# From block 13 on, score matmuls on 64x64 tiles that leave out the band's two empty quarters; an exp per key half; other due times

## The chip, the cores and the metric

The kernel runs on 1 core of one Trainium2 chip. The metric is device microseconds of that core for one execution. A core has TensorE (PE) for matmuls, VectorE (DVE), ScalarE (ACT), GpSimd (POOL) and SyncE (SP); POOL and SP issue the DMAs here. The profile names TensorE's weight loads apart, as PEld.

## The reference

Sliding-window attention with a linear distance bias, and a two-layer MLP with a squared ReLU on its result. B = 8, H = 8, S = 576, D = 64, window = 128; x is [4608, 512], the MLP is 512 -> 2048 -> 512.

```python
scores = scale * np.matmul(q, k.transpose(0, 1, 3, 2))
mask = (rel >= 0) & (rel < window)              # rel = query - key
scores = np.where(mask, scores - slope[h] * |rel|, -1e9)
attn = softmax(scores)
x = (attn @ v), heads side by side              # [4608, 512]
h = x @ w_in;  g = relu(h) ** 2;  out = g @ w_out
```

A block of 128 queries needs two blocks of keys: its own (keys not after the query) and the one before (keys less than 128 back). In the own block, keys 64..127 meet no query 0..63; in the block before, keys 0..63 meet no query 64..127. These are the band's two empty 64x64 quarters.

## The kernel before

**Blocks.** A batch has 576 tokens: four blocks of 128 and one of 64, 40 blocks in all, numbered m = 5 * b + kb. For each block, `load_block` (L338) loads k, q and v as bf16 with three POOL DMAs (L356) into the rings `kq` (8 buffers) and `vt` (8). `turn` (L388) transposes k and q into `kqT` (5 buffers): on TensorE for the blocks of `KQ_PE` (L425, with an evacuation by L373 on DVE or L375 on ACT), by a DMA transpose on SP's queue (L398) for the others.

**Scores.** `score` (L441) computes the scores transposed: keys on PSUM partitions, queries on columns. One head has contraction 64, so the two heads of a pair sit in the two row halves of the array. For each of the four pairs c, for each of the two key blocks, for each half, there is one 64-row matmul with 128 key columns as weights and 128 query columns as moving operand (L469): 16 matmuls a block. The 64-token last block of a batch is scored together with the first block of the next ("pair", 24 matmuls). The results go to four PSUM banks of pool A. A bank (`slot_s[i]`) takes two heads, and for each head 256 columns: key part 0 (block before), then part 1 (own). For each bank, ACT computes exp into a P buffer, 128 x 512 (L488), and DVE multiplies it with the mask exp(-slope * distance), zero outside the band (L496).

**Values.** `mix` (L500) multiplies P with v; a 65th column of ones gives the row sums (L516, 8 matmuls for each half of the heads, one bank each). DVE takes the reciprocal (L539) and normalizes into `x` (L544). x is transposed into `xT` on TensorE for the blocks of `X_PE` (L562), by a DMA transpose on SP (L554) for the others.

**MLP.** For each of nine groups g of 512 tokens, `fc_step` (L590) does 64 matmuls of 512 columns (L604) in steps of four, each step followed by ReLU on ACT (L613) and a square on DVE (L620); `t_part` (L655) does 64 matmuls with w_out (L665). A finished 128x512 tile is evacuated by ACT (L636) and stored by SP or POOL (L644). MLP matmuls use the four banks of pool B; scores, P times v and most transposes use the four banks of pool A.

**The order of work.** Every piece of work is a task with an engine, a planned cost, a key (due time), dependencies, and the slots that it takes and frees. `Plan.order` (L59) runs a list schedule over planned costs and fixes the order on each engine; the chip then runs each engine's list in order, waiting where data or a buffer is missing. A block's key is its place in the token stream less `AHEAD[m]` (L193, default `LEAD` or 0). `fill` (L712) puts matmuls on zeros (L705, L707) where the plan has TensorE idle in the first 26 us, `FILL` of the gap; `WARM` (L311) puts 24 ahead of all. `HOLD` and `OSB` (L202) say how long stores are held back and how many output buffers there are. Exp and mask take the key parts from the first one in use (`lo // 128`) to the last.

```python
at = 128 * i + 64 * part if pair and i == 0 else 128 * part          # L453
tm = plan.add({"PE": 220.0 + C * sum(max(w[2], 64) / 2.4 + 4 for w in work_of)}, due - 28, burst, ...)
te = plan.add({"ACT": act(cols)}, due - 28 + 3 * i, expo, [tm], [], [slot_s[i]])
```

Of the kernel before, what the change touches and what calls it, by code (L numbers as in the profile page):

```python
# [10 lines left out]
AF = mybir.ActivationFunctionType  # L11
ALU = mybir.AluOpType
# [158 lines left out]
def kernel(  # L171
    ctx: ExitStack, tc: tile.TileContext, q, k, v, moe_w_in, moe_w_out, out
):
    nc = tc.nc
# [5 lines left out]
    scale = 1.0 / (D ** 0.5)  # L180
# [4 lines left out]
    C = d_model // 128  # L185
# [4 lines left out]
    FIRST = "b0 b1 b2 i0 i1 i2 b3 i3 o0 b4 b5 o1 b6 b7 o2 o3 b8 b9"  # L190
    SPLIT = {0: [(0, 128), (128, 256), (256, 384), (384, 512)], 1: [(0, 192), (192, 512)]}
    EARLY = -80
    AHEAD = {10: -60, 1: 60, 4: 90, 9: -60, 5: -60, 0: -30, 12: 60, 11: 90, 2: 60, 8: 90, 7: 60, 6: 0, 3: -30, 24: 30, 14: 0, 18: 30, 25: 0, 23: 30, 16: -30, 13: 30, 21: 0, 19: -30}  # L193
    LEAD = 20

    KQ_PE = [0, 1, 2, 3, 4, 5, 6, 7, 8, 9]
    X_PE = [0, 1, 2, 3, 4, 5, 7, 8, 12, 17]
    WARM = 24
    FILL, UNTIL = 0.8, 26e3
    COLD = 0  # L200
    BANKS = {"A": 4, "B": 4}
    HOLD, OSB = 12, 14  # L202

    const = ctx.enter_context(tc.tile_pool(name="const", bufs=1))
    psum = ctx.enter_context(tc.tile_pool(name="psum", bufs=2, space=bass.MemoryType.PSUM))
# [3 lines left out]
    ident32 = const.tile([128, 128], FP32)  # L209
    kq32 = const.tile([128, 2, d_model], FP32)  # L210
    zero = const.tile([128, 128], BF16)
    masks = const.tile([128, H, 2, 128], BF16)
    pair_masks = const.tile([128, H, 256], BF16)
    dist = const.tile([128, 2, 128], FP32)
# [5 lines left out]
    def ring(name, n, shape):  # L220
        return [const.tile(shape, BF16, name=f"{name}_{i}") for i in range(n)]


    size = {"kq": 8, "v": 8, "kqT": 5, "P": 2, "x": 4}
    kq = ring("kq", size["kq"], [128, 2, d_model])
    vt = ring("vt", size["v"], [128, H, D + 1])
    kqT = ring("kqT", size["kqT"], [128, 2 * C, 128])
    Pt = ring("P", size["P"], [128, H, 2, 128])
    xt = ring("x", size["x"], [128, d_model])

    plan = Plan({"rec": 4, "rt": 3, "g": 2, "osb": OSB, **size}, BANKS, COLD)
    banks = {tag: [psum.tile([128, 512], FP32, name=f"{tag}_{i}", bufs=1) for i in range(n)] for tag, n in BANKS.items()}

    def act(n):
        return n * 0.84 + 55.0

    def dve(n, rate=1):
        return n / rate / 0.96 + 72.0
# [3 lines left out]


    def build_iota():
        nc.gpsimd.iota(dist, pattern=[[-128, 2], [1, 128]], base=128, channel_multiplier=-1,
                       allow_small_or_imprecise_dtypes=True)

    t_iota = plan.add({"POOL": 360.0}, -9.1e5, build_iota)

    def build_ident():  # L250
        nc.vector.tensor_single_scalar(ident32, dist[:, 1], 0.0, op=ALU.is_equal)
        nc.vector.tensor_copy(ident, ident32)

    t_ident = plan.add({"DVE": 350.0}, -9e5 - 1, build_ident, [t_iota])

    def build_dist():
# [9 lines left out]
    def place(h):  # L266
        c, half = divmod(h, 2)
        return 4 * (c // 2) + 2 * half + c % 2
# [11 lines left out]
        nc.vector.tensor_copy(pair_masks[:, :, 0:128].rearrange("p h (t s) -> p h t s", t=2), masks[:, :, :, 0:64])  # L280

    def pair_own():
        nc.vector.tensor_copy(pair_masks[:, :, 128:256], masks[:, :, 1, :])  # L283

    t_pair = [plan.add({"DVE": 340.0}, -9e5 + 9, f, later + t_mask) for f in (pair_rest, pair_own)]

    def ones():
# [21 lines left out]
    def warm():  # L309
        for i in range(WARM):  # L310
            nc.tensor.matmul(bank(sw)[:, 0:128], zero, zero, start=True, stop=True)  # L311
    sw = Slot("A")
    plan.add({"PE": 53.5 * WARM}, -9.1e5, warm, [t_ones], [sw], [sw]).cols = 128 * WARM

# [62 lines left out]
    def where(m):  # L377
        b, kb = divmod(m, NKB)
        return b, kb, blk[kb], (b * S + kb * 128 + blk[kb]) / 4 - 192 - 40 - AHEAD.get(m, LEAD if m not in X_PE else 0), b == 0

    def bank(slot):
        if slot.tile is None:
            slot.tile = banks[slot.tag][slot.idx]
            if slot.turns:
                slot.tile = slot.tile.bitcast(BF16)
        return slot.tile

    def turn(m):  # L388
        if m in t_kq_of:
            return  # L390
        b, kb, n, due, first = where(m)
        kq_by_dma = m not in KQ_PE

# [47 lines left out]
    def score(ms):  # L441
        due = where(ms[0])[3]
        sP = Slot("P")
        t_P = []
        pair = len(ms) == 2
        slot_s = [Slot("A") for _ in range(4)]
        work_of = []
        for i, m in enumerate(ms):
            b, kb, n, _, first = where(m)
            parts_of[m] = ([(0, m - 1)] if kb else []) + [(1, m)]  # L450
            P_of[m] = (sP, t_P)
            for part, mk in parts_of[m]:
                at = 128 * i + 64 * part if pair and i == 0 else 128 * part  # L453
                at_of[m, part] = at
                rel = [sk_of[mk]] if part == 0 or kb == NKB - 1 else []
                work_of.append((m, mk, n, at, rel))
        lo = min(w[3] for w in work_of)
        hi = max(w[3] + w[2] for w in work_of)
        n = 128 if pair else work_of[0][2]

        def burst():

            for sl in slot_s:
                bank(sl)
            for c in range(C):
                for m, mk, w, at, _ in work_of:
                    for half in range(2):
                        rows = slice(half * 64, half * 64 + 64)
                        nc.tensor.matmul(  # L469
                            slot_s[2 * (c // 2) + half].tile.rearrange("p (c x) -> p c x", c=2)[  # L470
                                :, c % 2, at:at + w],
                            kqT[sk_of[mk].idx][rows, c, :], kqT[sk_of[m].idx][rows, C + c, 0:w],
                            start=True, stop=True)
        tm = plan.add({"PE": 220.0 + C * sum(max(w[2], 64) / 2.4 + 4 for w in work_of)}, due - 28, burst,
                      [t for w in work_of for x in w[:2] for t in t_kq_of[x]] + chain["s"], slot_s + [sP],
                      [x for w in work_of for x in w[4]])
        chain["s"] = [tm]
        for i in range(4):
            def view(t):
                if pair:  # L480
                    return t
                return t.rearrange("p c (t q) -> p c t q", t=2)[:, :, lo // 128:2, 0:n]

            def Pv(i=i):
                return view(Pt[sP.idx][:, 2 * i:2 * i + 2].rearrange("p h t q -> p h (t q)"))

            def expo(i=i):
                nc.scalar.activation(Pv(i), view(slot_s[i].tile.rearrange("p (c x) -> p c x", c=2)),  # L488
                                     AF.Exp, bias=0.0, scale=scale)
            cols = 2 * sum(w[2] for w in work_of)  # L490
            te = plan.add({"ACT": act(cols)}, due - 28 + 3 * i, expo, [tm], [], [slot_s[i]])

            def mask(i=i):
                pt = Pv(i)
                mk = (pair_masks if pair else masks.rearrange("p h t q -> p h (t q)"))[:, 2 * i:2 * i + 2]
                nc.vector.tensor_tensor(pt, pt, view(mk), op=ALU.mult)  # L496
            t_P.append(plan.add({"DVE": dve(cols, 2)}, due - 28 + 3 * i, mask,
                                [te] + (t_pair if pair else [t_mask[h] for h in range(H) if place(h) // 2 == i])))

    def mix(m):  # L500
        b, kb, n, due, first = where(m)
        x_by_dma = m not in X_PE
        parts = parts_of[m]
# [68 lines left out]
    sk_of, t_kq_of, parts_of, P_of, at_of = {}, {}, {}, {}, {}  # L572
    m = 0
    while m < NBLK:
        ms = [m, m + 1] if m % NKB == NKB - 1 and m + 1 < NBLK else [m]
        for x in ms:
            turn(x)
        score(ms)
        for x in ms:
            mix(x)  # L580
        m += len(ms)
# [45 lines left out]
    LAST = [(0, 384), (384, 512)]  # L627
    odd = (2 + NBLK - len(KQ_PE) + NBLK - len(X_PE) + NG * 4 + 1) % 8

# [71 lines left out]
    def filler(slot, n):  # L701
        def emit():
            for i in range(n):
                if slot.turns:
                    nc.tensor.transpose(bank(slot)[:, 0:128], zero, ident)  # L705
                else:
                    nc.tensor.matmul(bank(slot)[:, 0:128], zero, zero, start=True, stop=True)  # L707
        t = Task({"PE": 107.0 * n / 2}, 0, emit, [t_ones, t_ident], [slot])
        t.eng, t.start, t.end, t.seq, t.cols = "PE", 0.0, 0.0, 0, 128 * n
        return t  # L710

    def fill(tasks):  # L712
        at, out = 0.0, []
        for t in tasks:
            if t.eng == "PE":
                slots = [s for s in t.acq if s.tag in BANKS]
                if slots and at and t.start < UNTIL:
                    n = int((t.start - at) * FILL / (107.0 if t.start < COLD else 54.0))
                    if n > 0:
                        out.append(filler(slots[0], n))  # L720
                at = t.start + t.engs["PE"] * (2 if t.start < COLD else 1)
            out.append(t)
# [36 lines left out]
```

The softmax here doesn't subtract the row's maximum and nothing guards it: scores larger than these inputs give would overflow.

## Time and profile before

| what | value |
|---|---|
| median of 7 runs | 312.63 us (312.26 to 313.02) |
| the profiled execution's own time | 313.02 us |
| its span, first to last instruction | 311.3 us |
| PE busy | 305.9 us (98%), 2824 matmuls |
| ACT busy | 179.2 us (58%) |
| DVE busy | 165.3 us (53%) |
| POOL busy | 107.3 us (34%) |
| granted TensorE clock, mean | 1.00 |

A row of the timeline has the start, the time from the first start to the last end of the merged instructions, engine, line, operation, output and inputs, the shape as rows * columns of weights and the moving operand, and how many. A matmul's duration (0.22 us for 128 columns, 0.38 us for 512) is longer than the distance to the next start (0.056 and 0.216 us), because they are pipelined: the cost of a matmul on TensorE is the distance between starts, and all sums use that.

### The profile page before, as it was taken

The page shows a single profiled execution, that of the slowest core. Times are in us where ns is not written, and L with a number is a line of the kernel's source. Part 1 is how long each engine was busy: PE and PEld are TensorE (multiplying, and loading weights), DVE is VectorE, ACT ScalarE, POOL GpSimd, SP SyncE. Part 2 cuts the span into 40 slices and gives each one's busy share as a digit, 9 for nine tenths or more (in the row PEclk, how much of TensorE's full clock was granted, in tenths as well). Part 3 has the DMA queues.
Part 4 walks back from the last instruction along what each step waited for, and adds up shares of the span by engine and source line. Part 5 has one row for each costly group of instructions (what it writes and reads, how often), then busy time and mean ns, then how long its engine had stood idle before and what let it go on. Part 6 is the DMA issues. An engine that isn't in the chain of part 4 may idle for free.

```text
span 311.3 us, 7179 instructions
## 1 busy us (share of the span) xinstructions
PE 305.9 (98%) x2824; PEld 173.9 (56%) x2824; DVE 165.3 (53%) x482; ACT 179.2 (58%) x342; POOL 107.3 (34%) x134
## 2 busy tenths in 40 slices
PE   8899999999999999999999999999999999999996
PEld 8799868675555555555454544445444454444443
DVE  5777666566557867676265555556455542222200
ACT  3777747585467847666455656665456654444411
POOL 8844958776455355447515120100000000000100
DMA  9999999999999999999999994766422120000021
GB/s 134 180 190 180 172 180 134 163 137 148 140 139 159 121 157 143 147 174 154 204 200 187 140 200 119 137 127 103 128 87 84 53 59 34 37 34 35 34 97 73
DMA packets 168114, 39.86 MB, mean 128 GB/s; under 512 B 159440, under 2 KB 163792, under 8 KB 168080
## 3 DMA queue, kind: packets, MB, share of 16 engines
q0 software_dynamic: 114896, 18.88, 86.3%
q1 hardware_dynamic: 53184, 20.52, 36.1%
q8 instruction: 22, 0.36, 0.4%
q14 instruction: 12, 0.10, 0.1%
HBM read 36.70 MB, written 9.44 MB: 148 GB/s over the span
## 4 chain that ended last, share of the span: by engine, by line
PE 96%; ACT 1%; DVE 1%; issue 0%; DVEq 0%
PE B L604 41%; PE B L665 40%; PE A L469 6%; PE A L516 5%; PE A L311 1%; PE B L516 1%; ACT masks L273 1%; PE B L707 1%; PE A L425 1%; ACT kqT L375 1%; PE B L425 0%; DVE kqT L373 0%; PE B L562 0%; PE A L562 0%; DVE pair_masks L283 0%; PE B L408 0%
## 5 line engine op out<-in xcount | busy, mean ns | idle before, releaser
L604 PE MATMUL B<-xT,w_in_sb 128*128 128x512 bf16 (+3 forms) x832 | 147.3, 314 | 0.0
L665 PE MATMUL B<-w_out_sb,g 128*128 128x512 bf16 (+2 forms) x592 | 145.1, 373 | 0.0
L613 ACT ACTIVATE rt<-B 128x512 bf16<-128x512 f32 (+2 forms) x152 | 86.6, 584 | 73.4 <-PE B L604 71.1
L620 DVE TENSOR_TENSOR g<-rt 128x512 bf16<-128x512 bf16 (+2 forms) x152 | 61.2, 405 | 73.5 <-ACT rt L613 72.4
L604 PEld LDWEIGHTS <-w_in_sb 128*128 128x128 bf16 x832 | 66.7, 98 | 48.0
L665 PEld LDWEIGHTS <-g 128*128 128x128 bf16 x592 | 54.2, 98 | 55.9
L488 ACT ACTIVATE P<-A 128x512 bf16<-128x512 f32 (+1 forms) x132 | 69.4, 590 | 19.3 <-PE A L469 19.3
L496 DVE TENSOR_TENSOR P<-P,masks 128x512 bf16<-128x512 bf16 (+1 forms) x104 | 42.4, 412 | 25.7 <-ACT P L488 22.3
L356 POOL DMA_DIRECT2D kq<-in_k_dram x39 | 33.3, 854 | 44.6 <-DMA kqT<-kq 31.2
L356 POOL DMA_DIRECT2D vt<-in_v_dram x40 | 34.3, 860 | 39.7 <-PE A L516 30.5
L356 POOL DMA_DIRECT2D kq<-in_q_dram x39 | 33.4, 857 | 12.6 <-DMA vt<-in_v_dram 4.3
L636 ACT ACTIVATE osb<-B 128x512 f32<-128x512 f32 (+1 forms) x36 | 21.6, 600 | 23.9 <-PE B L665 23.6
L516 PEld LDWEIGHTS <-P 128*128 128x128 bf16 x576 | 26.8, 98 | 14.8 <-DVE P L496 0.5
L644 POOL DMA_DIRECT2D out_dram<-osb x3 | 1.7, 563 | 89.5 <-ACT osb L636 89.5
L544 DVE TENSOR_TENSOR x<-A,rec 128x256 bf16<-128x256 f32 (+1 forms) x70 | 28.8, 418 | 1.3
L516 PE MATMUL A<-vt,P 128*128 128x65 bf16 x504 | 25.8, 193 | 0.0
L469 PEld LDWEIGHTS <-kqT 64*128 64x128 bf16 x576 | 14.9, 94 | 13.1 <-issue 11.9
L469 PE MATMUL A<-kqT,kqT 64*128 64x128 bf16 (+1 forms) x256 | 17.9, 212 | 1.1 <-DVE kqT L373 0.9
L469 PE MATMUL A<-kqT 64*128 64x128 bf16 (+1 forms) x320 | 18.4, 211 | 0.0
L539 DVE RECIPROCAL rec<-A 128x4 f32<-128x4 f32 (+1 forms) x70 | 12.1, 179 | 11.7 <-PE A L516 10.8
L496 DVE TENSOR_TENSOR P<-P,pair_masks 128x512 bf16<-128x512 bf16 x28 | 11.7, 420 | 6.7 <-ACT P L488 5.6
L638 DVE COPY osb<-B 128x128 f32<-128x128 f32 x1 | 0.3, 291 | 13.7 <-PE B L665 13.7
(48 smaller groups left out, 81.9 us busy)
## 6 DMA issues: line engine op xcount, KB each, us to landing
out_dram<-osb SPq DMA_DIRECT2D x32, 256.0 KB, 2.3
vt<-in_v_dram POOLq DMA_DIRECT2D x32, 128.0 KB, 8.3
kq<-in_k_dram POOLq DMA_DIRECT2D x31, 128.0 KB, 7.3
kq<-in_q_dram POOLq DMA_DIRECT2D x31, 128.0 KB, 7.9
w_in_sb<-in_moe_w_in_dram POOLq DMA_DIRECT2D x4, 512.0 KB, 10.2
w_out_sb<-in_moe_w_out_dram POOLq DMA_DIRECT2D x4, 512.0 KB, 9.2
out_dram<-osb POOLq DMA_DIRECT2D x3, 256.0 KB, 2.4
kq<-in_k_dram POOLq DMA_DIRECT2D x8, 64.0 KB, 9.7
```

What stands on the lines that cost most here:

```text
L356: nc.gpsimd.dma_start(o, src[b, :, kb * 128:kb * 128 + n, :].rearrange("h s d -> s h d"))
L469: nc.tensor.matmul(slot_s[2 * (c // 2) + half].tile.rearrange("p (c x) -> p c x", c=2)[:, c % 2, at:at + w], kqT[sk_of[mk].idx][rows, c, : ...
L488: nc.scalar.activation(Pv(i), view(slot_s[i].tile.rearrange("p (c x) -> p c x", c=2)), AF.Exp, bias=0.0, scale=scale)
L496: nc.vector.tensor_tensor(pt, pt, view(mk), op=ALU.mult)
L516: nc.tensor.matmul(bank(slot_v)[:, hi * (D + 1):(hi + 1) * (D + 1)], Pt[sP.idx][:, place(h)].rearrange("p t q -> p (t q)")[:, at_of[m, par ...
L539: nc.vector.reciprocal(srec.tile[0:n, :], pv[0:n, :, D])
L544: nc.vector.tensor_tensor(xt[sx.idx][0:n, hf * 256:(hf + 1) * 256].rearrange("p (h e) -> p h e", h=4), pv[0:n, :, 0:D], srec.tile[0:n, :]. ...
L604: nc.tensor.matmul(bank(slot)[:, fi * w:(fi + 1) * w], w_in_sb[:, cc, fc * 128:(fc + 1) * 128], xT[:, cc, g * 512 + lo:g * 512 + hi], star ...
L613: nc.scalar.activation(srt.tile[:, 0:cols], slot.tile[:, 0:cols], AF.Relu, bias=0.0, scale=1.0)
L620: nc.vector.tensor_tensor(sg.tile[:, fcs[0]:fcs[-1] + 1, lo:hi], r, r, op=ALU.mult)
L636: nc.scalar.activation(so.tile[:, lo:hi], slot.tile[:, lo:hi], AF.Copy)
L665: nc.tensor.matmul(bank(slot)[:, lo:hi], sg.tile[:, fc, t * 128:(t + 1) * 128], w_out_sb[:, fc, lo:hi], start=fc == 0, stop=fc == FCB - 1)
```

## The change

- `QUARTERS = 13`: the bursts of single blocks from 13 on with two key blocks of 128 (blocks 13, 16 to 18, 21 to 23, 26 to 28, 31 to 33, 36 to 38: 16 of the 33 bursts) issue for each pair c, each key part and each half two matmuls on 64x64 tiles: the full 128 queries for one key half, 64 queries for the other. That is 32 matmuls instead of 16, with 64 weight columns each; the two empty quarters are not computed.
- In those bursts each bank's exp is two ACTIVATEs on 64 partitions (key half 0 on columns 0..191, key half 1 on columns 64..255, of both heads). So that each is one stretch, the own block's columns now stand ahead of the block before: the masks' iota, the identity's and the pair masks' source and the `at` offsets follow. The mask multiplication still takes 128x512.
- The planned costs of these bursts and exps are changed accordingly.
- Block 9's k and q are transposed by DMA and not on TensorE; block 13's x on TensorE and not by DMA. `kq` has 7 buffers, not 8. `AHEAD`, `LEAD`, `WARM`, `FILL`, `HOLD`, `OSB` have other values.

```diff
-    AHEAD = {10: -60, 1: 60, 4: 90, 9: -60, 5: -60, 0: -30, 12: 60, 11: 90, 2: 60, 8: 90, 7: 60, 6: 0, 3: -30, 24: 30, 14: 0, 18: 30, 25: 0, 23: 30, 16: -30, 13: 30, 21: 0, 19: -30}
-    LEAD = 20
-
-    KQ_PE = [0, 1, 2, 3, 4, 5, 6, 7, 8, 9]
-    X_PE = [0, 1, 2, 3, 4, 5, 7, 8, 12, 17]
-    WARM = 24
-    FILL, UNTIL = 0.8, 26e3
+    AHEAD = {10: -30, 1: 0, 4: 30, 9: -60, 5: -30, 0: -30, 12: 30, 11: -30, 2: 90, 8: 60, 7: 90, 6: 30, 3: 90, 24: 30, 14: -60, 18: 30, 25: 60, 23: 30, 16: -30, 13: 60, 21: 0, 19: 0, 15: 90, 20: 60, 22: 0}
+    LEAD = 40
+
+    KQ_PE = [0, 1, 2, 3, 4, 5, 6, 7, 8]
+    X_PE = [0, 1, 2, 3, 4, 5, 7, 8, 12, 13, 17]
+    WARM = 16
+    FILL, UNTIL = 0.9, 26e3
     COLD = 0
+    QUARTERS = 13
     BANKS = {"A": 4, "B": 4}
-    HOLD, OSB = 12, 14
+    HOLD, OSB = 8, 10
...
-    size = {"kq": 8, "v": 8, "kqT": 5, "P": 2, "x": 4}
+    size = {"kq": 7, "v": 8, "kqT": 5, "P": 2, "x": 4}
...
-        nc.gpsimd.iota(dist, pattern=[[-128, 2], [1, 128]], base=128, channel_multiplier=-1,
+        nc.gpsimd.iota(dist, pattern=[[128, 2], [1, 128]], base=0, channel_multiplier=-1,
...
-                at = 128 * i + 64 * part if pair and i == 0 else 128 * part
+                at = 64 * (1 - part) if pair and i == 0 else 128 if pair else 128 * (1 - part)
...
+        quarters = not pair and len(work_of) == 2 and n == 128 and ms[0] >= QUARTERS
...
-            for c in range(C):
+            for c in range(C) if quarters else ():
+                m = ms[0]
+                for part, key_half, q0, q1 in ((1, 0, 0, 128), (1, 1, 64, 128), (0, 1, 0, 128), (0, 0, 0, 64)):
+                    mk = m - 1 + part
+                    ks = slice(key_half * 64, key_half * 64 + 64)
+                    for half in range(2):
+                        rows = slice(half * 64, half * 64 + 64)
+                        at = (c % 2) * 256 + at_of[m, part]
+                        nc.tensor.matmul(
+                            slot_s[2 * (c // 2) + half].tile[ks, at + q0:at + q1],
+                            kqT[sk_of[mk].idx][rows, c, ks], kqT[sk_of[m].idx][rows, C + c, q0:q1],
+                            start=True, stop=True)
+            for c in () if quarters else range(C):
...
-        tm = plan.add({"PE": 220.0 + C * sum(max(w[2], 64) / 2.4 + 4 for w in work_of)}, due - 28, burst,
+        tm = plan.add({"PE": 220.0 + (C * 88.0 if quarters else C * sum(max(w[2], 64) / 2.4 + 4 for w in work_of))},
+                      due - 28, burst,
...
             def expo(i=i):
+                for ks, lo, hi in ((slice(0, 64), 0, 192), (slice(64, 128), 64, 256)) if quarters else ():
+                    nc.scalar.activation(
+                        Pt[sP.idx][ks, 2 * i:2 * i + 2].rearrange("p h t q -> p h (t q)")[:, :, lo:hi],
+                        slot_s[i].tile[ks, :].rearrange("p (c x) -> p c x", c=2)[:, :, lo:hi],
+                        AF.Exp, bias=0.0, scale=scale)
+                if quarters:
+                    return
...
-            te = plan.add({"ACT": act(cols)}, due - 28 + 3 * i, expo, [tm], [], [slot_s[i]])
+            te = plan.add({"ACT": 2 * act(384) if quarters else act(cols)}, due - 28 + 3 * i, expo, [tm], [], [slot_s[i]])
```

More of the change, by code (lines that the diff above doesn't have):

```diff
@@ L250, in build_ident @@
     def build_ident():
-        nc.vector.tensor_single_scalar(ident32, dist[:, 1], 0.0, op=ALU.is_equal)
+        nc.vector.tensor_single_scalar(ident32, dist[:, 0], 0.0, op=ALU.is_equal)
         nc.vector.tensor_copy(ident, ident32)
@@ L282, in pair_own @@
     def pair_own():
-        nc.vector.tensor_copy(pair_masks[:, :, 128:256], masks[:, :, 1, :])
+        nc.vector.tensor_copy(pair_masks[:, :, 128:256], masks[:, :, 0, :])
     t_pair = [plan.add({"DVE": 340.0}, -9e5 + 9, f, later + t_mask) for f in (pair_rest, pair_own)]
@@ L457, in score @@
         lo = min(w[3] for w in work_of)
-        hi = max(w[3] + w[2] for w in work_of)
+        hi = max(w[3] for w in work_of) // 128 + 1
         n = 128 if pair else work_of[0][2]
+        quarters = not pair and len(work_of) == 2 and n == 128 and ms[0] >= QUARTERS
         def burst():
@@ L481, in view @@
                     return t
-                return t.rearrange("p c (t q) -> p c t q", t=2)[:, :, lo // 128:2, 0:n]
+                return t.rearrange("p c (t q) -> p c t q", t=2)[:, :, lo // 128:hi, 0:n]
             def Pv(i=i):
```

## The prediction

> **What bounds the kernel now.** I read the page's busy shares first, then TensorE's waits, then the timeline of score bursts, then ACT's groups by shape.
>
> ```profile
> PE 305.9 (98%) x2824; PEld 173.9 (56%) x2824; DVE 165.3 (53%) x482; ACT 179.2 (58%) x342; POOL 107.3 (34%) x134
> ...
> PE   8899999999999999999999999999999999999996
> ```
>
> TensorE is busy in every slice; only the first two and the last are lower. A busy PE need not do useful work, so the next view, all waits of PE in the span, matters more:
>
> ```profile
> PE A L311 <- DVE vt L290: 1.0, 1, 1.0
> PE A L469 <- DVE kqT L373: 0.9, 1, 0.9
> PE B L516 <- DVE P L496: 0.4, 1, 0.4
> ```
>
> All three lie before 15 us. From 40 us to 300 us every 20 us window shows 20.00 us of PE busy, at granted clock 1.00. So the time is the start-up plus the sum of TensorE's own steps, and a change counts by what it does to that sum, or by a wait that it makes where there is none. One score burst of 16 matmuls in the timeline (block 26):
>
> ```profile
> 154.02 0.38 PE L604 MATMUL B<-xT,w_in_sb 128*128 128x512 bf16 x1
> 154.34 0.23 PE L469 MATMUL A<-kqT,kqT 64*128 64x128 bf16 x2
> 154.40 0.22 PE L469 MATMUL A<-kqT 64*128 64x128 bf16 x2
> ...
> 154.74 0.22 PE L469 MATMUL A<-kqT 64*128 64x128 bf16 x2
> 154.89 0.82 PE L604 MATMUL B<-xT,w_in_sb 128*128 128x512 bf16 x3
> ```
>
> Eight pairs start from 154.34 to 154.74, 0.057 us apart: the two heads of a pair, in the two row halves of the array, run at the same time (a merged row of two lasts 0.23 us, one alone 0.22 us). The switch costs 0.10 us going in (154.02 + 0.216 = 154.24, first start 154.34) and 0.09 us coming out (154.74 + 0.057 = 154.80, next start 154.89). A burst costs 154.89 - 154.24 = 0.65 us, of which 8 x 0.057 = 0.46 us is streaming. A pair burst shows that streaming goes by columns:
>
> ```profile
> 141.44 0.19 PE L469 MATMUL A<-kqT,kqT 64*128 64x64 bf16 x2
> 141.47 0.25 PE L469 MATMUL A<-kqT 64*128 64x64 bf16 x4
> 141.55 0.19 PE L469 MATMUL A<-kqT,kqT 64*128 64x64 bf16 x2
> ```
>
> One c of it streams 64 + 64 + 128 columns in 0.11 us, so 64 columns take 0.028 us and 128 take 0.057 us, each with its own weight load hidden.
>
> **The change part by part.**
>
> *Quartered bursts.* The built order of the changed kernel has 512 matmuls on 64 weight columns: 16 bursts of 32. One c goes now from 2 x 0.057 = 0.114 us to a cost that no row shows, since no matmul here has 64 weight columns. Bounds:
> - Best: the two column halves run side by side as the two row halves do. Each tile then streams 128 + 64 columns for each c: 0.085 us. Saved: 4 x (0.114 - 0.085) = 0.116 us a burst, x 16 = 1.9 us.
> - Loads half hidden: the four f32 transposes at 6.71 us (L408) start every 0.11 us (6.71 to 7.15) where bf16 ones start every 0.056 us; if all of 0.11 us were the load of 128 weight columns, 64 columns take 0.055 us. That hides behind a 128-column matmul, not behind a 64-column one: 0.057 + 0.055 = 0.112 us for each c, saving 0.1 us in all 16 bursts.
> - Column halves one after the other: 128 + 64 + 128 + 64 columns, 0.170 us for each c: lost 4 x 0.056 = 0.22 us a burst, 3.6 us in all.
> - Worst: 0.085 us plus four unhidden loads of 0.055 us: 0.305 us for each c, 0.76 us a burst, 12 us in all. Eight P-times-v matmuls with 128-column bf16 loads start from 158.39 to the next work at 158.63, 0.030 us each, so a load of twice the width hides behind 65 columns there; this end is far from the nearest rows.
>
> I take 0.088 us, near the best, because the nearest rows are the row halves of the same instruction: two tiles, two loads, two matmuls with nothing lost but 0.003 us. Saved: 4 x (0.114 - 0.088) x 16 = **1.7 us**. The switches stay as they are, two for each burst, 0.19 us.
>
> Two rules of the Trainium skill speak against this. "TensorEngine Tiling (Array Packing)", section "Restrictions", says that column tiling disables the fast weight load, and "TensorE: Matmul & The Clock Gate", section "LDWEIGHTS (loading the stationary operand)", gives columns / 1.2 ns: 53 ns for 64 columns, by which one c takes an estimated 110 ns and the gain would be 0.3 us. The latter page's "The mechanism" says that matmuls start and end strictly in program order; if a 64-column matmul may not end ahead of the 128-column one before it, one c takes 114 ns and nothing is gained. No row here shows either.
>
> *Exps.* A 512-column exp takes ACT 0.49 us from start to start:
>
> ```profile
> 154.77 1.08 ACT L488 ACTIVATE P<-A 128x512 bf16<-128x512 f32 x2 [0.81 <-PE A L469]
> 155.75 0.60 ACT L613 ACTIVATE rt<-B 128x512 bf16<-128x512 f32 x1
> ```
>
> For 384 columns ACT has these groups by shape:
>
> ```profile
> L613 ACT ACTIVATE rt<-B 128x512 bf16<-128x512 f32 x128 | 75.9, 606 | 67.6 <-PE B L604 66.5
> L613 ACT ACTIVATE rt<-B 128x384 bf16<-128x384 f32 x8 | 3.8, 509 | 2.3 <-PE B L604 2.2
> L636 ACT ACTIVATE osb<-B 128x384 f32<-128x384 f32 x1 | 0.5, 490 | 2.0 <-PE B L665 2.0
> ```
>
> 0.10 to 0.11 us less, so 0.385 us from start to start, if 64 partitions cost what 128 do. A bank goes from 0.49 to 0.77 us, a block from 1.97 to 3.08 us, all 64 banks together +18 us of ACT. ACT is busy 35.2 of 50 us between 91 and 141 us and 64.5 of 109 us from there to 250 us; with six and nine such blocks at +1.1 us it comes to about 42 of 50 and 74 of 109. It has the room on average, so it costs nothing, as long as the MLP's matmuls of pool B cover each longer exp chain. The cover is thin in places. A burst needs all four banks of pool A, so it waits for the last exp of the burst before. In the changed order, by the distances above, TensorE has 4.2 us of other work between bursts behind blocks 15, 17, 22 and 23, and 4.7 us behind 33. The chain of eight exps is 3.1 us, one or two ReLUs or evacuations between them 0.5 to 1.0 us, the first exp's wait for its matmuls and the last one's tail 0.3 us: 3.9 to 4.4 us. So TensorE may wait 0 to 0.2 us in each, more if ACT starts late: 0 to 2 us together. I take **0.3 us**. DVE's masks keep their 128x512.
>
> *Block 9 by DMA, block 13 by TensorE.* Eight transposes less (L425, 0.056 us each) and four more (L562): **-0.22 us**. Block 13 adds one 0.42 us copy on DVE, 53% busy. On SP one kqT transpose comes in and one xT transpose goes. DMA-made kqT landed 10 us before its burst at blocks 10 to 13, and never less than 3.2 us (block 25); one kq buffer less and stores from tile 8 instead of 12 take from that, but the transposes wait for kqT's five buffers (each is issued just after the burst that frees one), not for kq. I cost it at nothing; without that cover, one late kqT costs a few us (it took 6 to 10 us from issue to landing in this stretch).
>
> *Start-up.* The order of real work on TensorE is the same up to 24 us; the fillers differ: 16 + 26 instead of 24 + 17 before the first transpose (+1), then +1, +2, +2, +2, before block 1's score burst, later +3, +1, +1 and so on. One costs 0.107 us before the clock is up (first 24: 2.74 us), 0.056 us after. The first +6 delay block 1's transposes, which had no wait: 0.107 + 5 x 0.056 = 0.39 us; the next two fall into the 0.9 us wait, three into the 0.4 us wait, the rest adds 0.06 each. The range is 0 (data comes later than TensorE anyhow) to 0.8 us (21 more, 8 warm ones fewer). I take **+0.45 us**.
>
> *Tail.* The last 60 us hold no scores but MLP matmuls at 0.216 us; unchanged. All MLP matmuls are there as before, in another order.
>
> **Sum**: -1.7 + 0.3 - 0.2 + 0.45 = -1.15 us. The profiled execution took 313.02 us (span 311.3 and 1.7 around it), so 311.9 by it; it lies 0.39 above the median of 312.63. By the median: **311.5 us**.
>
> **Rivals.** About 0.2% (0.6 us) is what a measurement can tell from no change.
> 1. *No overlap gained* (loads half hidden, or matmuls that end in order): the first term is -0.1 instead of -1.7, the sum +0.43 us: 313.1 us. For it: no row has mixed 64- and 128-column matmuls on neighbouring tiles. Against it: the row halves overlap fully. Chance 0.17.
> 2. *Column halves in turn*: slower than before. The mechanism is in the 16 bursts, at one c: the other terms are +0.53 together, so from 0.114 - 0.53 / 64 = 0.106 us on nothing is won, and from 0.116 us on it is slower by over 0.2%; at 0.170 us it is +3.6 + 0.53 = +4.1: 316.8 us. For it: weights and queries of both column halves come from the same 64 partitions, which the row halves do not share. Against: the best row I have. Chance 0.17, with another 0.04 for loads that do not hide at all (up to 12 us).
> 3. *ACT becomes what the bursts wait for*: -1.7 is kept, but four or five bursts wait 0.4 us each, and P times v some: +2 us in place of 0.3: 313.2 us. For it: the 4.2 us gaps. Against: 42 of 50 us busy on average. Chance 0.10.
> 4. *It does not do what it says*: the order has the 512 small matmuls and 128 exps of 64 partitions, so nothing is left for this.
>
> The forecast has 0.52. Its own range is 310.6 (best tiles, no filler cost, no waits: -2.1) to 312.0. The range for 8 in 10 has to take in the second rival: 310.5 to 317.0; what is left out is mostly the unhidden loads and waits above that. Faster: the forecast and a small part of rival 1, 0.55. Same: most of rival 1 and part of rival 3, 0.18. Slower: rival 2, and the rest of 1 and 3, 0.27.
>
> **What would show it.** Right: in the timeline behind 80 us, the starts within a quartered burst come eight for each 0.09 us and the burst costs 0.55 us in place of 0.65; TensorE's waits stay at start-up; ACT's exps of 64x384 take about 0.5 us. Rival 1: a burst still at 0.65 us; rival 2: 0.85 us or more. Rival 3: waits of L475 or L538 on ACT or DVE between 90 and 140 us. The fillers: block 1's burst starts 0.4 us later than 11.64 us. I am wrong altogether if SP's DMAs let bursts wait for kqT.

## The result and the profile after

The changed kernel takes 314.86 us (median of 14 runs, 314.06 to 315.49) against 313.0 us for the kernel before (36 runs): 1.0059 times as long, 95% interval 1.005 to 1.0069. The forecast was 311.5 us and faster, so it was wrong in its sign. The profiled execution took 314.87 us, with a span of 313.1 us, 1.8 us longer than before. Two experiments below had one slow execution each (319.33 and 319.69 us), and their times are medians of the others.

The page's busy shares of the changed kernel:

```profile
PE 307.1 (98%) x3089; PEld 174.3 (56%) x3089; DVE 164.2 (52%) x482; ACT 205.4 (66%) x405; POOL 107.2 (34%) x134
...
PE   8899999999999999999999999999999999999996
```

TensorE looks as full as before. ACT has 26 us more, where 18 were expected. A quartered burst in the timeline (block 21):

```profile
123.76 1.46 PE L626 MATMUL B<-xT,w_in_sb 128*128 128x512 bf16 x6
125.15 0.24 PE L475 MATMUL A<-kqT 64*64 64x128 bf16 x4
125.21 0.22 PE L475 MATMUL A<-kqT,kqT 64*64 64x128 bf16 x4
125.26 0.22 PE L475 MATMUL A<-kqT 64*64 64x128 bf16 x4
...
125.47 0.22 PE L475 MATMUL A<-kqT,kqT 64*64 64x128 bf16 x4
125.63 2.77 PE L626 MATMUL B<-xT,w_in_sb 128*128 128x512 bf16 x12
```

Two rows make one c: four matmuls of the own block, then four of the block before. The first c takes 0.108 us, each one after it 0.088 us. The whole burst, with both switches, costs 0.571 us by the distances between starts, in all 16 of them, where a whole burst costs 0.650 us. So the bursts do bring 16 x 0.079 = 1.26 us.

The loss is in another place. TensorE's matmuls still wait little by the profile, which counts a wait only from the end of the pipelined matmul before; but the weight loads ahead of P times v now wait for DVE's masks. The row of the view of PEld's waits (total, times, longest), and the place in the timeline where one of them lies (block 21, the second half of its heads):

```profile
PEld L538 <- DVE P L518: 2.1, 9, 0.3
```

```profile
129.73 0.48 ACT L504 ACTIVATE P<-A 64x384 bf16<-64x384 f32 x1
...
130.25 0.43 DVE L518 TENSOR_TENSOR P<-P,masks 128x512 bf16<-128x512 bf16 x1 [0.25 <-ACT P L504]
130.41 0.67 PE L538 MATMUL A<-vt,P 128*128 128x65 bf16 x8
130.73 0.23 PEld L538 LDWEIGHTS <-P 128*128 128x128 bf16 x6 [0.21 <-DVE P L518]
```

Eight P-times-v matmuls take 0.67 us instead of 0.41. Neighbouring heads lie in the two banks of a half in turn, with two matmuls for each head; so two start at once, and the third waits until the mask of the half's second bank is done at 130.67. That mask waited for the last exp (129.73 to 130.21). By the distances between starts there are 14 waits ahead of or within P times v between 85 and 250 us: 0.08 to 0.40 us, eight of them 0.25 to 0.31. Twelve are for that mask; the other two end as an exp of the next block ends, so they are for a bank that it still reads. The kernel before has one, of 0.09 us at 52 us.

The ledger of the 1.8 us, all from distances between TensorE's starts: bursts -1.26; waits ahead of and within P times v after 40 us +3.0; the pair burst of blocks 34 and 35, in whose middle TensorE waits, +0.2; transposes -0.44 + 0.22; the start-up +0.07 (block 3's burst at 24.87 us instead of 24.80). Sum +1.8. The start-up itself differs from one execution to the next: in the nine kernels here that share the changed kernel's order of TensorE's work up to block 3's burst, that burst began between 23.85 and 24.89 us. So profiled executions are compared below from block 3's burst to the start of the last matmul: 283.36 us before, 285.14 us after.

Why are the exps late? ACT's groups by shape, then, in the timeline of ACT, the eight exps of block 18:

```profile
L504 ACT ACTIVATE P<-A 64x384 bf16<-64x384 f32 x128 | 61.7, 482 | 2.2 <-PE A L475 0.4
...
L510 ACT ACTIVATE P<-A 128x512 bf16<-128x512 f32 x60 | 31.9, 612 | 7.8 <-PE A L483 7.7
```

```profile
111.39 4.00 ACT L504 ACTIVATE P<-A 64x384 bf16<-64x384 f32 x8
115.41 0.60 ACT L658 ACTIVATE osb<-B 128x512 f32<-128x512 f32 x1
```

One lasts 0.48 us, as the 384-column rows of the kernel before had it (0.49 to 0.51). But (4.00 - 0.48) / 7 = 0.50 us lies from start to start: these exps do not overlap. Those of 512 columns last 0.61 us and start every 0.49. So a bank costs ACT 1.00 us, not the 0.77 of the prediction nor the 0.755 that the plan books. By an estimate from these, the chain of four banks ends 4 x (1.00 - 0.755) = 1.0 us later than the plan had it when it set P times v.

### The profile page after: what moved, and what is told of

It is laid out like the page before. It is cut to its first block, busy times and chain, and to the rows that moved or that the text cites. A ratio compares the mean times of both kernels' runs of the same rounds, so it can differ in the third digit from the quotient of the medians.

```text
span 313.1 us, 7783 instructions
## 1 busy us (share of the span) xinstructions
PE 307.1 (98%) x3089; PEld 174.3 (56%) x3089; DVE 164.2 (52%) x482; ACT 205.4 (66%) x405; POOL 107.2 (34%) x134
## 4 chain that ended last, share of the span: by engine, by line
PE 79%; ACT 12%; issue 4%; DVE 3%; DVEq 0%; ACTq 0%
PE B L626 33%; PE B L687 32%; ACT P L504 9%; PE A L538 4%; PE A L483 3%; ACT rt L635 2%; PE A L475 2%; DVE P L518 2%; PE B L729 1%; PE B L538 1%; ACT masks L274 1%; PE A L312 1%; ACT kqT L376 1%; PE A L426 1%; PE B L426 0%
## 5 line engine op out<-in xcount | busy, mean ns | idle before, releaser
L687 PE MATMUL B<-w_out_sb,g 128*128 128x512 bf16 (+2 forms) x592 | 146.8, 374 | 0.0
L626 PEld LDWEIGHTS <-w_in_sb 128*128 128x128 bf16 x832 | 67.8, 98 | 49.4
L687 PEld LDWEIGHTS <-g 128*128 128x128 bf16 x592 | 53.3, 98 | 53.0
L504 ACT ACTIVATE P<-A 64x384 bf16<-64x384 f32 x128 | 61.7, 482 | 2.2 <-PE A L475 0.4
L510 ACT ACTIVATE P<-A 128x512 bf16<-128x512 f32 (+1 forms) x68 | 34.4, 585 | 7.9 <-PE A L483 7.7
L538 PEld LDWEIGHTS <-P 128*128 128x128 bf16 x576 | 27.5, 98 | 17.8 <-DVE P L518 2.1
L538 PE MATMUL A<-vt,P 128*128 128x65 bf16 x504 | 27.4, 194 | 1.1 <-ACT P L510 0.2
L483 PEld LDWEIGHTS <-kqT 64*128 64x128 bf16 x320 | 7.8, 94 | 6.2 <-issue 5.5
L475 PEld LDWEIGHTS <-kqT 64*64 64x64 bf16 x512 | 6.5, 108 | 6.8 <-issue 6.8
L483 PE MATMUL A<-kqT,kqT 64*128 64x64 bf16 (+1 forms) x128 | 9.0, 205 | 0.9 <-DVE kqT L374 0.7
```

The costliest lines, as they stand in the source:

```text
L483: nc.tensor.matmul(slot_s[2 * (c // 2) + half].tile.rearrange("p (c x) -> p c x", c=2)[:, c % 2, at:at + w], kqT[sk_of[mk].idx][rows, c, : ...
L504: nc.scalar.activation(Pt[sP.idx][ks, 2 * i:2 * i + 2].rearrange("p h t q -> p h (t q)")[:, :, lo:hi], slot_s[i].tile[ks, :].rearrange("p ...
L538: nc.tensor.matmul(bank(slot_v)[:, hi * (D + 1):(hi + 1) * (D + 1)], Pt[sP.idx][:, place(h)].rearrange("p t q -> p (t q)")[:, at_of[m, par ...
L626: nc.tensor.matmul(bank(slot)[:, fi * w:(fi + 1) * w], w_in_sb[:, cc, fc * 128:(fc + 1) * 128], xT[:, cc, g * 512 + lo:g * 512 + hi], star ...
L687: nc.tensor.matmul(bank(slot)[:, lo:hi], sg.tile[:, fc, t * 128:(t + 1) * 128], w_out_sb[:, fc, lo:hi], start=fc == 0, stop=fc == FCB - 1)
```

## The experiments

Theory A: the split exps are to blame, through the length of ACT's chain. Rival B: the new due times put P times v too near the bursts. Rival C: the 64x64 tiles slow the exps. All ratios below are to the kernel before, measured on the same chip side by side with it.

**One exp for each bank.**

```diff
-                for ks, lo, hi in ((slice(0, 64), 0, 192), (slice(64, 128), 64, 256)) if quarters else ():
-                    nc.scalar.activation(...)
-                if quarters:
-                    return
                 nc.scalar.activation(Pv(i), view(...), AF.Exp, bias=0.0, scale=scale)
...
-            te = plan.add({"ACT": 2 * act(384) if quarters else act(cols)}, ...)
+            te = plan.add({"ACT": act(cols)}, ...)
```

> The changed kernel with its quartered bursts, but with one exp of 128 x 512 for each bank, planned as before; the two empty quarters get the exp of what the bank held before, which the mask multiplies by zero. Theory A (the split exps are to blame: two of 64 partitions take ACT 0.99 us for a bank where one of 128 takes 0.49, so masks come late and P times v waits): the 3.2 us of waits go, the bursts stay at 0.57 us, time about 311.6, 1.3 us below the kernel before. Rival B (the new due times alone put P times v too close behind the bursts): waits stay, about 314.9.

311.0 us, ratio 0.9956 (0.9938 to 0.9973): as theory A expected, and faster than both kernels. From block 3's burst on it takes 282.09 us. The four exps behind block 18's burst in ACT's timeline, and P times v of block 21 in TensorE's:

```profile
111.14 2.06 ACT L508 ACTIVATE P<-A 128x512 bf16<-128x512 f32 x4 [0.79 <-PE A L475]
```

```profile
125.99 0.41 PE L536 MATMUL A<-vt,P 128*128 128x65 bf16 x8
...
127.10 0.41 PE L536 MATMUL A<-vt,P 128*128 128x65 bf16 x8
```

(2.06 - 0.60) / 3 = 0.49 us for a bank; half the ACT time of the split, though it computes the empty quarters too. Both halves of P times v take 0.41 us: no wait. Bursts still cost 0.571 us.

**No quarters.**

```diff
-    QUARTERS = 13
+    QUARTERS = 99
```

> The changed kernel with QUARTERS = 99, so no quartered burst and no split exp, all other edits kept. Theory A: no waits behind the start-up; 0.2 us less for the transposes of blocks 9 and 13, time 312.8, within 0.2% of before. Rival B: waits of 3 us stay and the bursts cost 0.65 us again, about 316.

312.47 us, 0.9993 (0.9984 to 1.0003): no waits of P times v after 40 us. The other edits (due times, rings, fillers, hold, transposes) together change nothing that can be measured in the time. With the run before: the quartered matmuls alone are worth 0.9956 / 0.9993, 0.4% or 1.2 us, which is their 1.26 us. Rival B falls.

**Split exps with whole bursts.**

```diff
-            for c in range(C) if quarters else ():
+            for c in ():
...
-            for c in () if quarters else range(C):
+            for c in range(C):
...
-        tm = plan.add({"PE": 220.0 + (C * 88.0 if quarters else C * sum(...))}, ...)
+        tm = plan.add({"PE": 220.0 + C * sum(...)}, ...)
```

> The changed kernel with whole score bursts (16 matmuls of 128 weight columns) but with the split exps. Theory A: bursts 0.65 us, ACT still 0.49 us from start to start of a 64-partition exp, waits of 3 us: 314.9 + 1.25 = 316.1. If the 64x64 tiles were what slows the exps (rival C), the exps overlap again, 0.39 us from start to start, and the time falls to about 313.

314.81 us, 1.0068 (1.0055 to 1.0082). The exps keep their 0.50 us from start to start, so the tiles have no part in it, and rival C falls. But the time is that of the changed kernel, not 1.25 us more, which I had expected of theory A: P times v waits 2.1 us here and 3.0 there. Where ACT's chain sets when P times v can go on, a shorter burst means that TensorE arrives there earlier: the last mask of block 31 ends 6.0 us after the burst's first start in both kernels, and the wait for it is 0.24 us here, 0.31 there. In the two profiled executions 0.9 of the 1.26 us turn into waits of P times v, and 0.07 into a longer wait in the pair burst; from block 3's burst on, the changed kernel is only 0.25 us shorter (285.14 against 285.39 us). The medians (314.81 and 314.86 us) are too coarse for that.

**Quarters and split exps with the due times of before.** The values of `AHEAD`, `LEAD`, `KQ_PE`, `X_PE`, `WARM`, `FILL`, `HOLD`, `OSB` and `kq` go back to those of the kernel before; `QUARTERS`, tiles and exps are as changed.

> The quartered bursts and split exps with the due times, rings, fillers and hold of the kernel before. Theory A: the exps are as late as in the changed kernel, waits of 2 to 4 us, time 313.5 to 315.5. Rival B: no waits, bursts 0.57 us, about 311.8.

315.88 us, 1.0091 (1.007 to 1.0112), runs from 314.25 to 316.27. The profiled one has 2.5 us of waits ahead of and within P times v. Right behind the bursts of blocks 17 and 18 an MLP matmul waits another 0.8 us, once for a ReLU (0.2 us) and once for a square (0.6 us). Theory A's direction, with 0.4 us above its range; the new due times were a little better for the split than the old ones, not worse.

**What keeps the exps apart.** Two kernels were made for this: both exps of a bank on all 128 partitions; and the order of the halves turned in every second bank.

```diff
-                for ks, lo, hi in ((slice(0, 64), 0, 192), (slice(64, 128), 64, 256)) if quarters else ():
+                for ks, lo, hi in ((slice(0, 128), 0, 192), (slice(0, 128), 64, 256)) if quarters else ():
```

> The changed kernel with both exps of a bank on all 128 partitions and the same 2 x 192 columns each (the empty quarters get the exp of what the bank held; the columns between are written twice). If it is the 64 partitions that keep an exp from overlapping the next (theory D): 0.39 us from start to start, 0.78 for a bank, near the planned 0.755, waits of P times v under 1 us, time 311.0 to 312.0. If it is the shape of 2 x 192 columns (rival E): 0.50 us stays, waits of 3 us, 314.9.

```diff
-                for ks, lo, hi in ((slice(0, 64), 0, 192), (slice(64, 128), 64, 256)) if quarters else ():
+                for ks, lo, hi in ((slice(0, 64), 0, 192), (slice(64, 128), 64, 256))[::1 - 2 * (i % 2)] if quarters else ():
```

> The changed kernel with the order of the two key halves turned round in every second bank, so that from bank to bank the partitions stay the same. If the change of partitions is what keeps exps apart (theory F): 0.39 us between two exps of one half, 0.50 where the half changes, waits of 2 us, 313.5. If any exp of 64 partitions is followed late (theory D): 0.50 us everywhere, time as the changed kernel, 314.9.

The first: 311.73 us, 0.9964 (0.9949 to 0.998). Four exps of block 21, two for each of two banks:

```profile
125.41 1.91 ACT L504 ACTIVATE P<-A 128x384 bf16<-128x384 f32 x4
```

By the single starts in the trace, an exp starts 0.388 us after the one before it from bank to bank, so the shape of 2 x 192 columns overlaps. Within a bank it starts 0.516 us after, 0.03 us behind the end of the first, some of whose columns it writes again (0.516 + 0.388 + 0.516 and the last one's 0.49 make the 1.91). A bank costs 0.90 us, 0.1 less than the split, and the waits of P times v are all but gone (0.1 us).

The second: 312.41 us, 0.9989 (0.9977 to 1.0001). The eight exps behind the same burst as above:

```profile
111.04 3.60 ACT L504 ACTIVATE P<-A 64x384 bf16<-64x384 f32 x8 [0.58 <-PE A L475]
```

(3.60 - 0.48) / 7 = 0.45 us, a mean of two: by the single starts in the trace it is 0.48 to 0.50 us where the half changes within a bank, and 0.387 to 0.391 us where the next bank begins with the same half. A 128-partition instruction behind half 0 follows in 0.387 us, behind half 1 in 0.51; and half 1 behind a 128-partition instruction, which comes nine times, follows in 0.62 us, behind an end at 0.59 to 0.60. So neither the 64 partitions nor the change of width cost anything; the overlap is lost when the next instruction starts on another partition (0 or 64) than the one before. That is theory F, in a sharper form. The waits of P times v go down from 3.0 to 0.9 us. They are longer than with two exps on all partitions, although eight exps in a row take less (3.60 against 3.73 us): the nine places where half 1 follows a ReLU or an evacuation without overlap lie ahead of a block's second or last bank.

**A longer chain without a change of partitions.** One exp of 128 x 512 into a spare buffer, then the real one.

```diff
+                if quarters:
+                    nc.scalar.activation(spare[i], slot_s[i].tile, AF.Exp, bias=0.0, scale=scale)
                 nc.scalar.activation(Pv(i), view(...), AF.Exp, bias=0.0, scale=scale)
```

> The changed kernel's order, but each quartered bank gets two exps of 128 x 512, the first into a spare buffer that nothing reads: no change of partitions, but the same 0.98 us of ACT for a bank. If the length of ACT's chain alone makes P times v wait (theory A): waits of about 3 us at the second mask of a half, as in the changed kernel, 314.5 to 315.2. If the 64 partitions hurt in another way, through masks or PSUM: no waits, 311.5.

314.79 us, 1.0064 (1.0049 to 1.008): the changed kernel's time. The same chain in ACT's timeline, then the row of PEld's waits:

```profile
125.18 0.59 ACT L510 ACTIVATE spare<-A 128x512 bf16<-128x512 f32 x1
125.66 0.60 ACT L511 ACTIVATE P<-A 128x512 bf16<-128x512 f32 x1
126.13 0.62 ACT L510 ACTIVATE spare<-A 128x512 bf16<-128x512 f32 x1
```

```profile
PEld L539 <- DVE P L519: 2.4, 9, 0.3
```

0.95 us for a bank, nine waits for the mask as in the changed kernel, and even the pair burst of blocks 34 and 35 waits its 0.2 us. The length of ACT's chain is enough to make the loss.

How closely the wait follows the chain shows in block 31 of five kernels with the changed due times and quartered bursts. In the last four of them a ReLU and an evacuation stand among its exps:

| exps of a bank | last mask ends, after the burst's first start | P times v waits |
|---|---|---|
| one | 3.12 us | 0 |
| two on 128 partitions | 5.76 us | 0.06 us |
| two halves, order turned in every second bank | 5.89 us | 0.19 us |
| two halves (the changed kernel) | 6.00 us | 0.31 us |
| two whole ones | 6.06 us | 0.37 us |

In the last four, from 5.76 to 6.06 us, the wait grows by as much as the mask is later.

**Telling the plan the true price.**

```diff
-            te = plan.add({"ACT": 2 * act(384) if quarters else act(cols)}, ...)
+            te = plan.add({"ACT": 980.0 if quarters else act(cols)}, ...)
```

> The changed kernel, but the plan is told 0.98 us for a bank's two exps instead of 0.755, which is what they take. If the waits come from the plan's wrong price (P times v set too early): most of the 3.2 us go, 312.0 to 312.8. If ACT's chain is too long for the blocks' pace whatever the order: waits of 2 us or more stay, or turn up elsewhere, 313.5 to 315.

317.05 us, 1.0135 (1.0086 to 1.0183), runs from 314.31 to 318.99: neither expectation. The waits of P times v do go (after 40 us none is left, apart from the step below and what follows it up to 148 us), so the plan's wrong price is what put P times v too early. But in its new order one MLP step waits for an x transpose by DMA:

```profile
138.77 1.24 PE L687 MATMUL B<-w_out_sb,g 128*128 128x512 bf16 x5
144.77 1.01 PE L626 MATMUL B<-xT,w_in_sb 128*128 128x512 bf16 x2 [4.75 <-DMA xT<-x]
```

4.75 us by the profile, 4.9 by the starts, more than all that was won; and behind it the granted clock is 0.57 on average from 144.77 to 148.00 us, with matmuls of 512 columns 0.42 us apart, which costs another 1.3 us. Without this one wait and its tail the profiled execution would have taken about 317.05 - 4.9 - 1.3 = 310.8 us, an estimate from its own rows, and as little as with one exp. What made the shorter executions shorter no trace shows. Whether due times that match the right price would get there was not tried, and stays open.

**One exp with the due times of before.**

> Quartered bursts with one 128 x 512 exp for each bank, and due times, rings, fillers and hold of the kernel before: the bursts alone. Theory A: 16 x 0.078 = 1.25 us less than before and no new waits, 311.4. If the new due times matter for the gain of the run with one exp: 312 or more.

312.44 us, 0.9991 (0.9978 to 1.0004). The bursts cost 0.571 us and P times v does not wait longer than before, but one MLP step waits 0.9 us at 114.7 us, and at 30.5 us transposes wait 0.5 us for a load of q. So the gain of the bursts alone does not come through in an order that was made for other costs; in the new order it does.

**One exp, quarters from block 6 on.** As the first run, with `QUARTERS = 6`.

> Quartered bursts with one exp for each bank from block 6 on instead of 13 (blocks 6, 7, 8, 11 and 12 too). Theory A: five more bursts at 0.571 instead of 0.65 us, 0.4 us less than the 311.0 us of the run with one exp from block 13: 310.6. If the early blocks wait for loads or evacuations anyway, the gain turns into waits: 311 or more.

311.66 us, 0.9963 (0.995 to 0.9977). All five bursts go down to 0.571 us and P times v shows no waits, yet the time is not below the first run's; the intervals of both overlap widely, and the two profiled executions reach block 1's burst 1.1 us apart (10.53 and 11.63 us) without a difference in what stands before it. The medians cannot show a gain of 0.4 us. The traces do: from block 6's burst to the start of the last matmul it is 264.25 us with quarters from block 13 on and 263.86 us with quarters from block 6 on, 0.39 us less.

## Why the prediction was wrong

- **What bounds the kernel.** Right: the time moved by TensorE's own steps and by waits that were not there before. The ledger of the two profiled executions closes.
- **Quartered bursts, -1.7 us.** The mechanism was right: the column halves run side by side, one c takes 0.088 us as I took it. Its size was 1.26 us, because the first c takes 0.11 us and the last matmuls are followed by 0.13 us of their own end and the switch. Neither of the two rules that I had weighed against it made itself felt: loads of 64 columns at 53 ns would have made one c 110 ns, ends in strict order 114 ns; 88 were measured. Rivals 1 and 2 fall with that.
- **Exps: the step that failed.** "0.385 us from start to start, if 64 partitions cost what 128 do" measured 0.50 us. The duration was right (0.48); the overlap with the next instruction, which I had taken over from rows that all start on partition 0, was not there. ACT's 18 us more became 26 us of busy time, and a block's chain 4.0 us instead of 3.08. By that the waits, for which I had taken 0.3 us and at most 2, became 3.2 us: 3.0 at P times v and 0.2 at a burst. With two exps on all partitions a bank costs 0.90 us, more than the 0.77 that I had reckoned with, and P times v waits 0.1 us: at 0.77 the term of 0.3 us would have been enough.
- **Where the waits lie.** I looked for them at the bursts, which wait for all four banks, and priced P times v with "and P times v some". In fact one burst waited, and P times v 14 times, most of them because the third matmul of a half needs a mask that comes a bank later than the first one's. This is rival 3 by its mechanism, with 0.10 of chance, at one and a half times its price. I had read the average, 42 of 50 us of ACT, as a reason against it: measured 43.7 of 50. The average was nearly right and said nothing about a chain that has to end in time.
- **Start-up, +0.45 us.** Not settled. Block 1's burst began at 11.64 us in both profiled executions and block 3's 0.07 us later than before; but in the nine kernels with this order of the start-up block 1's burst began anywhere from 10.53 to 11.66 us, and in the three with the old one from 10.35 to 11.64. A term of 0.45 us cannot be read from that.
- **Transposes of blocks 9 and 13, -0.22 us, and kqT by DMA at no cost.** Right: -0.44 and +0.22, by the number of transposes and their 0.056 us; the least time from a landed kqT to its burst is 4.1 us (3.2 before).

With no new waits, my sum with the measured sizes would have been -1.26 - 0.22 + 0.07 = -1.4 us. The run with one exp, which has no such waits, comes to -1.4 us by its ratio (-0.8 to -1.9 by the interval), and from block 3's burst on to 283.36 - 282.09 = 1.27 us less than before.

## What to carry to other kernels

Less arithmetic on an engine off the critical path can cost time there if it comes as more instructions: two exps that together do three quarters of the work took twice as long as one whole exp, and the full exp over columns that a mask zeroes anyway was the better one. Before relying on a chain on another engine, count its length from start to start for just the sequence that will run, with who follows whom, and set it against the work that covers it at the tightest place; an average share of busy time does not tell. A list schedule follows its prices: a wrong one moves waits into the fixed order, and a better one may open another wait elsewhere.

## What the runs showed of the hardware

- ACT instructions overlap their follower by 0.10 to 0.12 us if it starts on the same partition, with 64 partitions as with 128 (64x384 then 64x384 of the same half: 0.388 us from start to start at 0.485 us each; 64 partitions from 0, then 128: 0.387; 128x512: 0.49 at 0.61), and by nothing if it starts on another one (64x384: 0.48 to 0.51 us at 0.485; 128x512, then 64 partitions from 64: 0.62 at 0.60). The Trainium skill's "ScalarE: Activation LUTs", section "What ACT_TABLE_LOAD costs", gives an overlap of about 93 ns for back-to-back instructions; the runs here agree for the first case and differ for the second.
- An exp that writes again some of what the exp before it wrote starts behind its end: 0.516 us instead of 0.388. Reading the same bank is not the reason: two whole exps of one bank into different buffers start 0.48 us apart at 0.60.
- Matmuls on four 64x64 tiles stream at 0.088 us for 128 + 64 columns on each tile, with a weight load for every matmul; going into that mode costs 0.09 us and out of it 0.10, about what the 64x128 one costs (0.10 and 0.09).
- After TensorE had waited 4.9 us, the granted clock was 0.57 on average for the next 3.2 us, with matmuls of 512 columns 0.42 us apart instead of 0.216 (the run with the plan's true price).
